# Split weights kept in DRAM for the second half, and every second sum of the second product on ScalarE in two convolution stages

## The chip, the core and the metric

The kernel runs on one core of one Trainium2 chip. The metric is the device time of that core in microseconds (us). Engines are called as in the profile: PE (TensorE), PEld (its weight loads), DVE (VectorE), ACT (ScalarE), POOL (GpSimd), SP (SyncE, which here only issues transfers).

## The reference

One sequence of S = 2048 rows of D = 576 channels. x is normalized by rows, and the output is x plus two branches of the normalized rows: a long convolution with gates (H3), and a two-layer network with ReLU whose hidden width is 4608.

```python
def A(q, k, v, shift_k, ssm_k, ssm_D):
    k_shift = sum of k shifted by 0..3 rows, each times a row of shift_k
    kv = k_shift * v
    y = irfft(rfft(pad(kv)) * rfft(pad(ssm_k)))[:S]     # along the rows, by channel
    return q * (y + kv * ssm_D)
def B(x, w1, w2):
    return relu(x @ w1) @ w2                            # 576 -> 4608 -> 576
xn = layernorm(A_q)
return A_q + A(xn, A_k, A_v, A_shift_k, A_ssm_k, A_ssm_D) + B(xn, B_w1, B_w2)
```

## The kernel before

**The network.** The rows are handled in two halves of 1024, each of two blocks of 512 (`HB` = 2) with four tiles of 128 rows (`BT` = 4). Each half runs over 18 chunks of 256 hidden columns (`NCHUNK`), so there are 36 chunks, `ci` 0 to 35, and chunk `ci` uses the same weights as chunk `ci + 18`. All products are of float32 numbers that are held as two parts, high and low (`hh` and `ll` for the hidden values); a product takes three matmuls: high x high, high x low, low x high.

The first product of a chunk is `quad` (chunks 0 and 18 take the plain form, `mm1`): it combines the four blocks of weights and x in the manner of Strassen and Winograd, in the banks `psk` (or `ka`), `pst` and `psa` of PSUM, and `relu` turns a finished bank into `hh` (on ACT) and `ll` (on DVE). The second product is `second`, run beside the next chunk's first product: for each of the two blocks one turn `mm2_rest` (4 matmuls of 512 columns, the last 64 output columns, transposed) and four turns `mm2` (6 matmuls each), ten turns a chunk. A turn takes one of the two banks of the pool `ps_o`, and DVE adds the finished bank to the sum held in SBUF (`accT` and `acc`). `DRAINS` says how many turns follow each step of `quad`.

**The weights of a chunk.** `prepare(ci)` runs one chunk ahead, in seven steps: DVE combines blocks of w1 (`combine_w`, four sums on the raw tile `r_`, lines 356 to 359); ACT rounds the main seven blocks to the high part and POOL subtracts for the low one (`split_main`, names `gah` and `gal`), then the same for two groups of the rest (`split_rest`, `gbh` and `gbl`) and two tiles of w2 (`split_w2`, `w_`). The raw loads of the next chunk stand after the fifth and the last step (`load_w1`, `load_w2`; one buffer each). All this is done in both halves.

**The convolution** is a generator, `conv`, of four stages: fk transforms the filter `ssm_k` (tile `kt`, loaded by 16 transfers), fx forms k, shift and v and transforms them (`tap`, `gate`, `split`), fm multiplies and transforms back along the other axis, from and to DRAM (`zk`, `zx`, `zy`), fo makes the last transform, the gate and the sum. Its matmuls have 288 columns and use the banks `psf`.

**Order.** PE's program sets the pace: after every third 512-column matmul `tick` advances a clock, and when the convolution's share is due it runs the stream on to its next `yield`. `yield -n` holds the stream back until n more matmul columns have been issued (16,000 columns, a `PAUSE`). `START` delays the stream's beginning, and `PAUSES` tells the rate how much holding back to reckon with. The program orders each engine's instructions by a model of their times, and places marked `issue_after` stay behind the named instruction: `here()` puts a convolution's step behind the last sum of the second product (`done["acc"]`) and the last activation (`done["act"]`).

**The start.** The four tiles of block 0 are loaded in two pairs; `first_xT` takes their statistics (BN_STATS, DVE), scales them (`normalized`) and transposes them on PE. `load_w1(0)` and `load_w2(0)` load chunk 0's weights; a part of them is held until the statistics of the first pair (`issue_after(seen.ins)`).

Of the kernel before, what the change touches and what calls it, by code (L numbers as in the profile page):

```python
# [10 lines left out]
F32 = mybir.dt.float32  # L11
# [6 lines left out]
P = 128  # L18
# [27 lines left out]
STEP = 3  # L46
DM = 512
DRAINS = (1, 1, 2, 1, 2, 2, 1)
SECOND = {(NCHUNK - 6, 0): 1, (NCHUNK - 4, 0): 0}
# [3 lines left out]
PAUSE = 16000  # L53
START = 24000
PAUSES = 24
SHARE = 0.985
# [61 lines left out]
def h3_ffn_kernel(ctx: ExitStack, tc, x, k, v, shift_k, ssm_k, ssm_D, w1, w2, fwd, inv, mid, out):  # L118
# [73 lines left out]
    def normalized(dst, src, t):  # L192
        nc.vector.tensor_scalar(dst, src, mv[:, t, 0:1], rstd[:, t:t + 1],
                                op0=OP.subtract, op1=OP.mult)

# [64 lines left out]
    def first_xT(srcs):  # L260

        plain_tiles(0)
        ps = []
        for c in range(5):
            ps.append(ps_o.tile([P, 512], F32, tag="o", name=f"psx{c}") if c >= 3 else fft_psum())
        xn = {}
        for t0 in range(0, BT, 2):
            pair = xp.tile([P, 2, D], F32, tag="xn", name=f"xn{t0}", bufs=BT // 2)
            for t in (t0, t0 + 1):
                seen = stats(t, srcs[t])  # L270
                xn[t] = pair[:, t % 2, :]
            if t0 == 0:
                with tc.issue_after(seen.ins):
                    load_w1(0, ((P, P),))
                    load_w2(0)
            inv_std(t0, 2)
            for t in (t0, t0 + 1):
                normalized(xn[t], srcs[t], t)
                for c in range(5):
                    w = min(P, D - c * P)  # L280
                    nc.tensor.transpose(ps[c][:w, t * P:(t + 1) * P], xn[t][:, c * P:c * P + w],
                                        ident)
                keep_warm(WARM_TILE[t])
        for c in range(5):
            split_x(0, c, ps[c])
# [59 lines left out]
    def load_w2(ci):  # L345
        f0 = (ci % NCHUNK) * FC
        r2 = wp.tile([P, FT, D], F32, tag="r2", name=f"r2_{ci}", bufs=1)
        nc.sync.dma_start(r2, w2[f0:f0 + FC, :].rearrange("(j p) d -> p j d", p=P))
        raw_w[2, ci] = r2
# [10 lines left out]

    def pair_of(tag, ci, n, bufs):
        return tuple(wp.tile([P, n, P], F32R, tag=f"{tag}{m}", name=f"{tag}{m}_{ci}", bufs=bufs)
                     for m in "hl")

    def split_main(ci):
        hi, lo = pair_of("ga", ci, 7, 2)
        src = raw_w[1, ci][:, :7, :]
        with at_turn(ci):
            nc.scalar.activation(hi, src, AF.Copy)  # L369
        split_lo(lo, src, hi)  # L370
        names = ("s1", "s2", "s3", "s4", "a12", "a22", "a11")
        weights[ci].update({n: (hi[:, k, :], lo[:, k, :]) for k, n in enumerate(names)})

    def split_plain(ci, j):
        if j == 0:
            weights[ci]["ga"] = pair_of("ga", ci, 7, 2)
        hi, lo = weights[ci]["ga"]
        src = raw_w[1, ci][:, 4 + j:8:2, :]
        to = slice(j, 4, 2)
        with at_turn(ci):  # L380
            nc.scalar.activation(hi[:, to, :], src, AF.Copy)
        split_lo(lo[:, to, :], src, hi[:, to, :])
        for k, n in ((j, "a12" if j == 0 else "a22"), (2 + j, "a11" if j == 0 else "a21")):
            weights[ci][n] = hi[:, k, :], lo[:, k, :]

    def split_rest(ci, j):
        hi, lo = pair_of("gb", f"{ci}_{j}", 3, 3)
        src = raw_w[1, ci][:, 8 + j::2, :]
        with at_turn(ci):
            nc.scalar.activation(hi, src, AF.Copy)  # L390
        split_lo(lo, src, hi)
        weights[ci]["r", j] = hi, lo

    def split_w2(ci, j):
        r2 = raw_w[2, ci]
        w = wp.tile([P, 2 * D], F32R, tag="w2", name=f"w2_{ci}_{j}", bufs=2 * FT)
        with at_turn(ci):
            nc.scalar.activation(w[:, :D], r2[:, j, :], AF.Copy)  # L398
# [3 lines left out]
        return last  # L402

    hid = {}
# [16 lines left out]
    def rest(ci, j, bi):  # L421
        hi, lo = weights[ci]["r", j]
# [58 lines left out]
    accT = {}  # L481

    def mm2_rest(ci, b):


        ps = ps_o.tile([P, 512], F32, tag="o", name=f"psr{ci}_{b}")
# [3 lines left out]
        if ci % NCHUNK == 0:  # L490
            accT[b] = xp.tile([P, 512], F32, tag="accT", name=f"accT{b}")
            done["acc"] = nc.vector.tensor_copy(accT[b], ps)
# [13 lines left out]
    def mm2(ci, b, i):  # L506
        t = b * BT + i
        cols = slice(i * P, (i + 1) * P)
        if ci == HALVES * NCHUNK - 1:
            while t not in added:  # L510
                next(stream)
        ps = ps_o.tile([P, 512], F32, tag="o", name=f"pso{ci}_{t}")
        seq = []
        for j in range(FT):
# [3 lines left out]
            seq += [(hh[:, cols], wh), (hh[:, cols], wl), (ll[:, cols], wh)]  # L518
        run_seq(ps, seq, True, True)
        last = ci == HALVES * NCHUNK - 1 and t == T - 1  # L520
        for d in range(2) if last else range(1):
            dc = slice(d * DM // 2, (d + 1) * DM // 2) if last else slice(0, DM)
# [34 lines left out]
    @contextmanager  # L557
    def here():


        with tc.issue_after(done["acc"].ins), tc.issue_after(done["act"].ins):
            yield

    def conv():

        with tc.tile_pool(name="fk", bufs=2) as fp:
            kt = fp.tile([P, NH, A2], F32, tag="kt", name="kt", bufs=1)  # L570
# [3 lines left out]
            for d in range(0, NH, KD):  # L574
                for h in range(2):
                    src = ssm_k[h * NH + d:h * NH + d + KD, :].rearrange("d (p t) -> p d t", t=A2)
                    nc.sync.dma_start(kt[halves(h)[0], d:d + KD, :], src)  # L577
                    yield -KT_GAP
# [33 lines left out]


        with tc.tile_pool(name="fx", bufs=2) as fp:
            sk = fp.tile([P, KS, D], F32, tag="sk", name="sk", bufs=1)
            for j in range(KS):
                nc.sync.dma_start(sk[:, j, :], shift_k[j:j + 1, :].to_broadcast([P, D]))
            win, gates, mats, sums, stks = {}, {}, {}, {}, {}
# [68 lines left out]


        with tc.tile_pool(name="fm", bufs=2) as fp:
            m_sb = fp.tile([P, 2, 2, P], F32R, tag="m", name="m_sb", bufs=1)  # L690
# [87 lines left out]


        with tc.tile_pool(name="fo", bufs=2) as fp:  # L780
            raw, parts, rest, ys = {}, {}, {}, {}
# [89 lines left out]


    stream = conv()
    clock = {"ffn": 0.0, "conv": 0.0, "until": START, "done": False}
# [50 lines left out]
    for j in range(FT):  # L925
        with tc.issue_after(done["act"].ins):
            done["pool"] = split_w2(0, j)
    load_w2(1)

    def prepare(ci):  # L930

        if ci >= HALVES * NCHUNK:
            while True:
                yield
        if ci % NCHUNK:
            combine_w(ci)
            yield
            split_main(ci)
        else:
            split_plain(ci, 0)  # L940
            yield
            split_plain(ci, 1)
        yield
        split_rest(ci, 0)
        yield
        split_rest(ci, 1)
        if ci + 1 < HALVES * NCHUNK:
            load_w1(ci + 1)
        yield
        split_w2(ci, 0)  # L950
        yield
        split_w2(ci, 1)
        if ci + 1 < HALVES * NCHUNK:
            load_w2(ci + 1)
        while True:
            yield

    def second(ci, half):
        for b in range(half * HB, (half + 1) * HB):
            mm2_rest(ci, b)  # L960
            yield
            for i in range(BT):
                mm2(ci, b, i)
                if i == 0 and ci % NCHUNK == NCHUNK - 1:
                    turn_back(b)
                yield

# [88 lines left out]
```

## Time and profile before

| | |
|---|---|
| median of 3 runs | 1173.7 us (1173.07 to 1176.47) |
| the profiled execution | 1176.29 us |
| its span, first to last instruction | 1174.5 us |
| mean granted clock of PE | 0.976 |
| busy: PE, DVE, ACT, POOL | 94%, 77%, 54%, 27% of the span |
| bytes by DMA | 151.81 MB |

A busy time is the time in which an engine has an instruction at work, and PE counts as busy also when its clock is throttled; "granted clock" is the share of full speed that it had. A line of waits reads: engine, tile and line of the instruction that waited, then what ended its wait, then total us, number, longest. In a line of single instructions the first column is the start in us, the second the duration, and what stands in brackets is the idle time before it and what ended it. A group of instructions reads: tile written and tiles read, shape out and in, count, then busy us and mean ns of one, then idle time before them and what ended most of it.

### The profile page before, as it was taken

To read this page: it belongs to the slowest core of one execution; us is meant where nothing else is said; L and a number is where in the kernel's file an instruction comes from. 1 tells how busy PE (TensorE), PEld (TensorE's weight loads), DVE (VectorE), ACT (ScalarE), POOL (GpSimd) and SP (SyncE) were. 2 spreads that over 40 slices of the span, in tenths; PEclk is the share of its full clock that TensorE was granted. 3 is DMA by queue.
4 is the path that set the end of the run, shared out by engine and by line. 5 is a ranking of instruction groups with operands and counts; after the bars stand their busy time and mean duration, and the time that the engine had idled before them with its cause. 6 is when DMAs were issued, how large, how long until landed. Compare 5 with 4: busy or idle time off the path is not lost.

```text
span 1174.5 us, 15018 instructions
## 1 busy us (share of the span) xinstructions
PE 1099.6 (94%) x5011; PEld 891.4 (76%) x5011; DVE 904.9 (77%) x1461; ACT 637.3 (54%) x1293; POOL 321.0 (27%) x328
## 2 busy tenths in 40 slices
PE   7799999998989999899999999999999998799997
PEld 5478888886767777678778888888788876578785
DVE  4844888768999989895777777777777765998985
ACT  2332677743434333324268887877788784544430
POOL 3233333322133333322132222221222221324520
PEclk8899999999899999999999999999999999899999
DMA  9941355464444445323464433434433424745723
GB/s 182 167 122 43 112 159 149 147 180 135 143 141 141 123 134 145 115 64 122 127 185 117 124 104 116 126 89 124 113 102 114 124 83 129 224 142 146 206 72 80
DMA packets 121016, 151.81 MB, mean 129 GB/s; under 512 B 46093, under 2 KB 71439, under 8 KB 120940
## 3 DMA queue, kind: packets, MB, share of 16 engines
q1 hardware_dynamic: 112652, 136.69, 42.3%
q0 software_dynamic: 7968, 13.44, 4.4%
q10 hardware_dynamic: 320, 0.74, 0.3%
q8 instruction: 39, 0.64, 0.2%
q14 instruction: 37, 0.30, 0.1%
HBM read 115.44 MB, written 35.39 MB: 128 GB/s over the span
## 4 chain that ended last, share of the span: by engine, by line
PE 58%; DVE 21%; ACT 7%; issue 5%; DMA 4%; SPq 3%; POOL 0%; DVEq 0%; ACTq 0%; POOLq 0%
PE pso L411 22%; PE psk L411 11%; PE psa L411 8%; PE pst L411 7%; PE psf L718 4%; PE psr L411 3%; DVE acc L523 3%; SPq L577 2%; DVE e L642 2%; DMA r<-in_w 2%; PE psf L554 2%; DVE ll L433 2%; DVE c L643 1%; DVE k L767 1%; ACT hh L432 1%
## 5 line engine op out<-in xcount | busy, mean ns | idle before, releaser
L411 PE MATMUL pso<-w,hh 128*128 128x512 f32 x1152 | 371.2, 402 | 38.0 <-DVE acc L523 28.4
L411 PEld LDWEIGHTS pso<-w,hh 128*128 128x128 f32 x1152 | 211.1, 191 | 91.3 <-DVE acc L523 38.4
L523 DVE TENSOR_TENSOR acc<-pso,acc 128x512 f32<-128x512 f32 x289 | 196.1, 681 | 51.8 <-PE pso L411 49.9
L411 PE MATMUL pso<-w,ll 128*128 128x512 f32 x576 | 229.3, 398 | 0.0
L324 POOL TENSOR_TENSOR gbl<-r,gbh 128x384 fp32r<-128x384 f32 x72 | 80.2, 1114 | 341.2 <-ACT gbh L390 332.9
L324 POOL TENSOR_TENSOR w<-r,w 128x512 fp32r<-128x512 f32 (+1 forms) x144 | 125.8, 904 | 162.6 <-ACT w L398 162.5
L411 PEld LDWEIGHTS pso<-w,ll 128*128 128x128 f32 x576 | 110.0, 191 | 23.8
L324 POOL TENSOR_TENSOR gal<-r,gah 128x896 fp32r<-128x896 f32 (+1 forms) x38 | 78.0, 2053 | 142.0 <-ACT gah L369 113.8
L548 DVE TENSOR_TENSOR ks<-kt,ks 64x288 fp32r<-64x288 f32 x64 | 49.2, 768 | 21.7 <-ACT ks L547 19.0
L369 ACT ACTIVATE gah<-r 128x896 fp32r<-128x896 f32 x34 | 32.4, 953 | 60.1 <-DVE r L359 59.9
L411 PE MATMUL psr<-hh,w 128*128 128x512 f32 x144 | 58.6, 407 | 5.7 <-DVE acc L523 4.8
L433 DVE SCALAR_TENSOR_TENSOR ll<-psk,hh 128x512 fp32r<-128x512 f32 x68 | 46.6, 685 | 21.3 <-ACT hh L432 21.0
L494 DVE TENSOR_TENSOR accT<-psr,accT 128x512 f32<-128x512 f32 x68 | 46.5, 684 | 19.4 <-PE psr L411 19.3
L411 PE MATMUL psr<-ll,w 128*128 128x512 f32 x144 | 58.4, 405 | 2.0 <-DVE ll L433 2.0
L432 ACT ACTIVATE hh<-psk 128x512 fp32r<-128x512 f32 x68 | 40.5, 595 | 30.8 <-PE psk L411 17.1
L709 DVE TENSOR_TENSOR lox<-ztx,hix 128x576 fp32r<-128x576 f32 x32 | 26.1, 817 | 39.4 <-ACT hix L708 39.4
L411 PE MATMUL psk<-xh,gbh 128*128 128x512 f32 x136 | 53.5, 393 | 0.0
L411 PE MATMUL psk<-xh,gbl 128*128 128x512 f32 x136 | 53.5, 393 | 0.0
L411 PE MATMUL psk<-xl,gbh 128*128 128x512 f32 x136 | 53.5, 393 | 0.0
L547 ACT ACTIVATE ks<-kt 64x288 fp32r<-64x288 f32 x64 | 47.3, 739 | 8.3 <-DVE kt L587 7.0
L398 ACT ACTIVATE w<-r 128x576 fp32r<-128x576 f32 x72 | 46.1, 676 | 6.3 <-DMA r<-in_w 4.0
L432 ACT ACTIVATE hh<-psa 128x512 fp32r<-128x512 f32 x35 | 20.8, 595 | 47.3 <-PE psa L411 47.0
(263 smaller groups left out, 2625.1 us busy)
## 6 DMA issues: line engine op xcount, KB each, us to landing
r<-in_w SPq DMA_DIRECT2D x36, 576.0 KB, 4.3
r<-in_w SPq DMA_DIRECT2D x35, 512.0 KB, 4.2
zk<-zk SPq DMA_DIRECT2D x32, 288.0 KB, 3.1
zx<-zx SPq DMA_DIRECT2D x32, 288.0 KB, 3.0
ztk<-zk SPq DMA_DIRECT2D x32, 288.0 KB, 2.8
ztx<-zx SPq DMA_DIRECT2D x32, 288.0 KB, 3.3
zy<-vo SPq DMA_DIRECT2D x32, 288.0 KB, 2.5
zo<-zy SPq DMA_DIRECT2D x32, 288.0 KB, 3.4
```

Of the source, the lines that this page charges most:

```text
L324: return nc.gpsimd.tensor_tensor(dst, src, hi, OP.subtract)
L369: nc.scalar.activation(hi, src, AF.Copy)
L398: nc.scalar.activation(w[:, :D], r2[:, j, :], AF.Copy)
L411: nc.tensor.matmul(ps, a, m, start=start and i == 0, stop=stop and i == len(seq) - 1, skip_group_check=not start)
L432: done["act"] = nc.scalar.activation(hh, ps, AF.Relu)
L433: lows.append(nc.vector.scalar_tensor_tensor(ll, ps, 0.0, hh, op0=OP.max, op1=OP.subtract))
L494: done["acc"] = nc.vector.tensor_tensor(accT[b], ps, accT[b], OP.add)
L523: done["acc"] = nc.vector.tensor_tensor(acc[t][:, dc], ps[:, dc], acc[t][:, dc], OP.add)
L547: nc.scalar.activation(dst[own], src[own], AF.Copy)
L548: nc.vector.tensor_tensor(dst[other], src[own], dst[own], OP.subtract)
L709: nc.vector.tensor_tensor(lo, raw[name, g], hi, OP.subtract)
L718: nc.tensor.matmul(ps[:, :NH], a, m[:, cols], start=n == 0, stop=n == 2)
```

## The change

Four things are changed.

1. **Kept weights.** In the first half each chunk's split weights are stored to DRAM (`kept_a`, `kept_b`, `kept_2`; five transfers a chunk on SP's queue, high and low part together, for which the tiles of the two parts become one tile). In the second half `prepare` loads them back (`fetch`), and `combine_w`, the splits and the raw loads fall away there.
2. **Seeds.** In the stages fx and fo (`SEEDED`), in all chunks but the first and last of a half, every second turn of the second product doesn't end in a sum by DVE: `prime` has ACT copy the sum from SBUF into the bank ahead of the matmuls, which add to it, and ACT copies the bank back. A turn's bank is taken one turn earlier.
3. **The filter's loads** are held back: each of the 16 has a memset of one column of its tile on DVE ahead of it, under `here()`. `START` falls from 24,000 to 8,000 columns and `PAUSES` rises from 24 to 25; the pause between fx's first loads and their use grows from 3 to 4 `PAUSE`, and these loads are put in another order (row of `sk`, then tile of k, by turns).
4. **The start.** The statistics of the second pair of tiles come after the scaling of the first (`issue_after(scaled.ins)`), and the held-back part of chunk 0's loads has three memsets of single columns ahead of it in place of `issue_after(seen.ins)`.

```diff
+SEEDED = ("fx", "fo")
-START = 24000
-PAUSES = 24
+START = 8000
+PAUSES = 25
...
+    kept_a = dram.tile([NCHUNK, P, 2, 7, P], F32, name="kept_a")
+    kept_b = dram.tile([NCHUNK, FT, P, 2, 3, P], F32, name="kept_b")
+    kept_2 = dram.tile([NCHUNK, FT, P, 2 * D], F32, name="kept_2")
...
-                seen = stats(t, srcs[t])
+                with tc.issue_after(scaled.ins) if t0 else nullcontext():
+                    stats(t, srcs[t])
...
-                with tc.issue_after(seen.ins):
-                    load_w1(0, ((P, P),))
-                    load_w2(0)
+                nc.vector.memset(raw_w[1, 0][:, 5, 0:1], 0.0)
+                nc.vector.memset(raw_w[1, 0][:, 13, 0:1], 0.0)
+                load_w1(0, ((P, P),))
+                load_w2(0)
...
+    def keep_main(ci):
+        n = 7 if ci else 4
+        nc.sync.dma_start(kept_a[ci, :, :, :n], f32(weights[ci]["ga"])[:, :, :n])
+    def keep_rest(ci):
+        for j in range(FT):
+            nc.sync.dma_start(kept_b[ci, j], f32(weights[ci]["r", j]))
+    def keep_w2(ci):
+        for j in range(FT):
+            nc.sync.dma_start(kept_2[ci, j], f32(weights[ci]["w2", j]))
+    def fetch(ci):
+        c0 = ci - NCHUNK
+        weights[ci] = {}
+        t = main_tile(ci)
+        n = 7 if c0 else 4
+        nc.sync.dma_start(f32(t)[:, :, :n], kept_a[c0, :, :, :n])
+        name_main(ci, t)
+        for j in range(FT):
+            yield
+            weights[ci]["r", j] = rest_tile(ci, j)
+            nc.sync.dma_start(f32(weights[ci]["r", j]), kept_b[c0, j])
+        for j in range(FT):
+            yield
+            weights[ci]["w2", j] = w2_tile(ci, j)
+            nc.sync.dma_start(f32(weights[ci]["w2", j]), kept_2[c0, j])
...
+    def seeded(ci):
+        return 0 < ci % NCHUNK < NCHUNK - 1 and stage[0] in SEEDED
+    def prime(ci, n):
+        b, i = ci // NCHUNK * HB + n // (BT + 1), n % (BT + 1)
+        ps = ps_o.tile([P, 512], F32, tag="o", name=f"pso{ci}_{b}_{i}")
+        seed = seeded(ci) and n % 2 == 1
+        if seed:
+            src = accT[b] if i == 0 else acc[b * BT + i - 1][:, :DM]
+            nc.scalar.activation(ps, src, AF.Copy)
+        turns[ci, n] = ps, seed
...
-        run_seq(ps, seq, True, True)
+        run_seq(ps, seq, not seed, True)
...
+        if seed:
+            done["act"] = nc.scalar.activation(acc[t][:, :DM], ps, AF.Copy)
+        for d in range(2) if last else range(0) if seed else range(1):
...
+                    with here():
+                        nc.vector.memset(kt[halves(h)[0], d:d + 1, 0:1], 0.0)
                     nc.sync.dma_start(kt[halves(h)[0], d:d + KD, :], src)
                     yield -KT_GAP
...
-            for t in range(1 - KS, 2):
-                load(t)
-            yield -3 * PAUSE
+            for j in range(KS):
+                nc.sync.dma_start(sk[:, j, :], shift_k[j:j + 1, :].to_broadcast([P, D]))
+                load(-j)
+            load(1)
+            yield -4 * PAUSE
...
     def prepare(ci):
-        if ci % NCHUNK:
+        if ci < NCHUNK:
             combine_w(ci)
+            keep_rest(ci - 1)
             yield
             split_main(ci)
             yield
             split_rest(ci, 0)
+            keep_w2(ci - 1)
             yield
             split_rest(ci, 1)
             if ci + 1 < NCHUNK:
                 load_w1(ci + 1)
             yield
             split_w2(ci, 0)
+            keep_main(ci)
             yield
             split_w2(ci, 1)
             if ci + 1 < NCHUNK:
                 load_w2(ci + 1)
+        elif ci < HALVES * NCHUNK:
+            ...
+            yield from fetch(ci)
```

How the instructions then stand is shown at three places. A row names line, operation, tile written and tiles read (the number behind a name tells one tile from the next), shape, and the count where rows of one kind follow each other.

First SP's queue of transfers at the start, behind chunk 0's weights. `acc` are rows of x, `kt` and `skip` the filter, `r_1` the raw weights of chunk 1. Before:

```order
L162 DMA acc_231<-in_x 64x1152 x2
L162 DMA acc_234<-in_x 64x1152 x2
L573 DMA skip<-in_ssm_D 1x288 x2
L577 DMA kt<-in_ssm_k 64x36x32 x11
L340 DMA r_1_237<-in_w 128x4x256
L342 DMA r_1_237<-in_w 64x256 x2
L577 DMA kt<-in_ssm_k 64x36x32 x2
L348 DMA r_1_249<-in_w 128x2x576
```

and now, with chunk 0's split weights (`ga_`, `gb_`, `w_0`) stored as well:

```order
L166 DMA acc_237<-in_x 64x1152 x2
L642 DMA skip<-in_ssm_D 1x288 x2
L429 DMA kept_b<-gb_0_136 128x768
L425 DMA kept_a<-ga_133 256x1x512
L346 DMA r_1_240<-in_w 128x4x256
L348 DMA r_1_240<-in_w 64x256 x2
L429 DMA kept_b<-gb_1_231 128x768
L433 DMA kept_94<-w_0_0_244 128x1152
L356 DMA r_1_253<-in_w 128x2x576
L433 DMA kept_94<-w_0_1_248 128x1152
L648 DMA kt<-in_ssm_k 64x36x32 x5
```

The raw weights of chunk 1 stood behind eleven of the filter's loads and now stand ahead of all of them, behind two stores.

Second ACT in stage fx, in chunk 10's first product. `hh` are the hidden values' high parts, `gbh`, `gah` and `w_10` (now `ga`, `gb`, `w_10`) the weights' splits, `zx` copies out of the convolution's banks. Before:

```order
L432 ACTIVATE hh_0_0_2925<-psk_2892 128x512
L390 ACTIVATE gbh_0_3011<-r_11_2799 128x384
L398 ACTIVATE w_10_0_2855<-r_10_2634 128x576
L398 ACTIVATE w_10_1_2886<-r_10_2634 128x576
L555 ACTIVATE zx_0_2834<-psf 128x288 x2
L555 ACTIVATE zx_1_2909<-psf 128x288 x2
L369 ACTIVATE gah_2977<-r_11_2799 128x896
L432 ACTIVATE hh_0_1_3033<-psa 128x512
```

and now:

```order
L480 ACTIVATE hh_0_0_2985<-psk_2952 128x512
L417 ACTIVATE w_10_0_2913<-r_10_2685 128x576
L588 ACTIVATE acc_237<-pso_1_4_2901 128x512
L417 ACTIVATE w_10_1_2946<-r_10_2685 128x576
L623 ACTIVATE zx_0_3048<-psf 128x288 x2
L543 ACTIVATE pso_0_1_2958<-acc_98 128x512
L623 ACTIVATE zx_1_3129<-psf 128x288 x2
L543 ACTIVATE pso_0_3_3020<-acc_101 128x512
L588 ACTIVATE acc_98<-pso_0_1_2958 128x512
L480 ACTIVATE hh_0_1_3097<-psa 128x512
L588 ACTIVATE acc_101<-pso_0_3_3020 128x512
L389 ACTIVATE ga_3055<-r_11_2856 128x896
```

Two copies into a bank of `pso` (L543) and three back (L588) came in between the hidden values' rows, and the main weight split (L389) moved behind the last of these.

Third DVE in stage fo, in chunk 31. `y` and `ll` belong to the convolution's last transform and to the hidden values, `r_32` is the raw tile that `combine_w` works on, `acc` the sum of the second product. Before:

```order
L859 TENSOR_TENSOR y_9230<-psf,low_1_9277 64x288
L433 SCALAR_TENSOR_TENSOR ll_0_0_9746<-psk_9705,hh_0_0_9745 128x512
L356 TENSOR_TENSOR r_32_9598<-r_32_9598 128x128
L357 TENSOR_TENSOR r_32_9598<-r_32_9598 128x128
L523 TENSOR_TENSOR acc_5253<-pso_15_9680,acc_5253 128x512
L469 TENSOR_TENSOR psk_9705<-psa,e_31_9778 128x512
L358 TENSOR_TENSOR r_32_9598<-r_32_9598 128x128
L859 TENSOR_TENSOR y_9230<-psf,low_1_9277 64x288
```

and now:

```order
L933 TENSOR_TENSOR y_9499<-psf,low_0_9500 64x288
L481 SCALAR_TENSOR_TENSOR ll_0_0_9591<-psk_9548,hh_0_0_9590 128x512
L514 TENSOR_TENSOR pst_9617<-psa,e_31_9621 128x512
L933 TENSOR_TENSOR y_9499<-psf,low_1_9552 64x288 x2
L559 TENSOR_TENSOR accT_5375<-pso_2_0_9565,accT_5375 128x512
L903 SCALAR_TENSOR_TENSOR acc_5332<-y_9400,rstd,acc_5332 128x576
L887 TENSOR_TENSOR olo_9609<-zo_9510,ohi_9608 128x576
L895 SCALAR_TENSOR_TENSOR y_9499<-xt_9329,mv,y_9499 128x576
L517 TENSOR_TENSOR psk_9548<-psa,e_31_9621 128x512
```

The rows of `r_32` are gone, and of the second product's sums only `accT` (L559) stands in this stretch; the convolution is a little further on.

More of the change, by code (lines that the diff above doesn't have):

```diff
@@ L421, in rest @@
     def rest(ci, j, bi):
-        hi, lo = weights[ci]["r", j]
+        hi, lo = (weights[ci]["r", j][:, m] for m in range(2))
         xh, xl, xr = plain[bi]
@@ L511, in mm2 @@
                 next(stream)
-        ps = ps_o.tile([P, 512], F32, tag="o", name=f"pso{ci}_{t}")
+        ps, seed = turns.pop((ci, b % HB * (BT + 1) + 1 + i))
         seq = []
@@ L558, in here @@
     def here():
-        with tc.issue_after(done["acc"].ins), tc.issue_after(done["act"].ins):
+        with tc.issue_after(done.get("acc", lows[-1]).ins), tc.issue_after(done["act"].ins):
             yield
     def conv():
+        stage[0] = "fk"
         with tc.tile_pool(name="fk", bufs=2) as fp:
```

118 lines of the change are left out of this document (67 added, 51 removed).

## The prediction, before the changed kernel was run

> **What bounds the kernel now.** I read the page first, then busy time by stretch, then PE's waits, then the timeline at the longest of them.
>
> ```profile
> span 1174.5 us, 15018 instructions
> PE 1099.6 (94%) x5011; PEld 891.4 (76%) x5011; DVE 904.9 (77%) x1461; ACT 637.3 (54%) x1293; POOL 321.0 (27%) x328
> ```
>
> PE is the busiest by far, so what counts is the time in which it isn't at full pace. The stretches (busy us of PE, PEld, DVE, ACT, POOL; then granted clock, DMA share, GB/s):
>
> ```profile
> 0.00:100.00 100.00, 85.06 (x336) 62.14 (x337) 54.94 (x119) 28.85 (x54) 29.89 (x36) 0.90 0.88 143
> 100.00:250.00 150.00, 148.54 (x693) 122.58 (x692) 112.07 (x168) 104.03 (x187) 47.14 (x52) 1.00 0.42 129
> 250.00:600.00 350.00, 318.79 (x1384) 254.87 (x1384) 297.84 (x461) 122.63 (x235) 97.72 (x96) 0.97 0.44 131
> 600.00:950.00 350.00, 345.25 (x1707) 291.67 (x1706) 262.62 (x423) 280.42 (x611) 84.73 (x75) 1.00 0.41 119
> 950.00:1150.00 200.00, 183.22 (x820) 146.28 (x819) 165.09 (x262) 101.36 (x208) 61.49 (x71) 0.97 0.50 141
> 1150.00:1174.50 24.50, 18.79 (x81) 13.81 (x79) 12.30 (x31) 0.00 (x0) 0.00 (x0) 0.99 0.36 96
> 300.00:350.00 50.00, 44.27 (x176) 34.75 (x177) 45.94 (x65) 18.41 (x35) 9.97 (x10) 0.90 0.49 151
> 350.00:400.00 50.00, 45.38 (x202) 36.15 (x201) 45.78 (x62) 18.21 (x36) 18.55 (x17) 1.00 0.39 121
> 1050.00:1100.00 50.00, 47.72 (x219) 38.93 (x220) 46.66 (x78) 24.45 (x48) 18.94 (x22) 1.00 0.64 175
> 1100.00:1150.00 50.00, 49.80 (x228) 40.71 (x227) 41.68 (x66) 17.88 (x36) 17.59 (x22) 1.00 0.33 99
> ```
>
> Lost PE time = idle + (1 - clock) x length: start 14.9 + 10 = 24.9; stage fk (100 to 250) 1.5; fx and the change of halves (250 to 600) 31.2 + 10.5 = 41.7; fm (600 to 950) 4.8; fo (950 to 1150) 16.8 + 6 = 22.8; tail 5.9. Together 101.6 us. The last three rows say where it comes from: with DVE at 45.8 or 46.7 of 50 us, PE idles 4.6 or 2.3; with DVE at 41.7 it idles 0.2; in fm, DVE at 37.5 of 50, it idles 0.7. The waits (total us, times, longest) name DVE too:
>
> ```profile
> PE pso L411 <- DVE acc L523: 28.4, 27, 2.5
> PE psr L411 <- DVE acc L523: 4.8, 1, 4.8
> ```
>
> The PE work itself, the same 3,955 matmuls of 512 columns (the code's counts, with the warming ones) and 960 of 288, doesn't change: starts stand 0.23 and 0.13 us apart at full pace, so about 3,955 x 0.233 + 960 x 0.133 + 6 for transposes = 1055 us.
>
> ```profile
> 985.79 0.29 PE L718 MATMUL psf<-yl,m_sb 128*128 128x288 f32 x1
> 985.92 0.30 PE L718 MATMUL psf<-yh,m_sb 128*128 128x288 f32 x1
> ...
> 986.32 0.39 PE L411 MATMUL psa<-t3h,gah 128*128 128x512 f32 x1
> 986.55 0.40 PE L411 MATMUL psa<-t3l,gah 128*128 128x512 f32 x1
> ```
>
> So each edit is worth what it takes out of the 101.6 us, at the stretch in which it acts, less what it adds.
>
> **The start.** Two things stand there.
>
> ```profile
> 1.09 0.06 DVE L907 MEMSET table<- 128x1 f32 x1
> 6.29 1.54 DVE L178 BATCH_NORM_STATS2 bn<-acc 128x6 f32<-128x288 f32 x4 [5.14 <-DMA acc<-in_x]
> ...
> 10.59 1.18 DVE L178 BATCH_NORM_STATS2 bn<-acc 128x6 f32<-128x288 f32 x3 [2.52 <-DMA acc<-in_x]
> 13.67 1.05 DVE L193 TENSOR_SCALAR xn<-acc,mv,rstd 128x576 f32<-128x576 f32 x2
> 14.38 0.87 PE L281 MATMUL psf<-ident,xn 128*128 128x128 f32 x3 [5.00 <-DVE xn L193]
> ...
> 18.24 0.63 PE L281 MATMUL psx<-ident,xn 128*128 128x128 f32 x2
> 20.46 19.43 SPq L577 DMA_DIRECT2D kt<-in_ssm_k  x8
> 40.08 1.98 SPq L340 DMA_DIRECT2D r<-in_w  x1
> 53.19 1.26 ACT L398 ACTIVATE w<-r 128x576 fp32r<-128x576 f32 x2 [4.00 <-DMA r<-in_w]
> 55.00 0.77 DVE L239 TENSOR_TENSOR t2l<-va,t2h 128x512 fp32r<-128x512 f32 x1 [2.74 <-ACT t2h L238]
> 56.75 1.22 PE L411 MATMUL pso<-w,hh 128*128 128x512 f32 x2 [4.01 <-DVE accT L492]
> ```
>
> (1) The first tiles are scaled only after the statistics of the late second pair (10.59). Now they are scaled before those, and PE transposes them early. The second pair's statistics take 1.5 from 10.59, and the small rows to its scaling 1.9 (from 11.77, the end of the statistics row, to 13.67 now); so its transposes start near 14.6 and, at about 1.1 us for each of two tiles, end near 16.8, not at 18.9: 2 us. The three memsets on the weights' tiles cost nothing: in the built order they stand ahead of everything that waits, so they hold no load back. (2) Eleven of the filter's loads stand on SP's queue ahead of chunk 1's weights, which were issued at 40.1; ACT waited for them until 53.2, DVE for ACT, PE for DVE. With each filter load behind a one-column memset on DVE (16 of 0.06 us, 1 us in all, spread over three chunks), chunk 1's weights are issued when their buffer is free, some 15 us earlier. That takes away DVE's 2.7 us and with it 3 of the 4.0; of the 10 us that the clock of 0.90 cost over this stretch I count 4 as given back. Start: 24.9 - 2 - 3 - 4 = 16. The filter loads now end nearer to their use (fk starts 16,000 columns, 7 us, earlier): 1 us more in fk, 2.5.
>
> **Kept weights.** First half: 5 stores a chunk, 2.9 MB, 51.5 MB in all; second half the same bytes back instead of 22.4 MB raw. 151.8 now + 103 - 22.4 = 232 MB, over 1131 us 205 GB/s. In fx that is 131 + 92 = 223 GB/s; at the 0.44 that 131 cost, 0.75 of the DMA engines. Nothing in the trace goes above 0.64 at 175 outside the start, so the landing time is bounded by 4.3 us (now) and 7.0 (the filter's, at the start's load); I take 5.
>
> ```profile
> DMA packets 121016, 151.81 MB, mean 129 GB/s; under 512 B 46093, under 2 KB 71439, under 8 KB 120940
> ...
> r<-in_w SPq DMA_DIRECT2D x36, 576.0 KB, 4.3
> kt<-in_ssm_k SPq DMA_DIRECT2D x16, 288.0 KB, 7.0
> ```
>
> Raw weights are issued about a chunk, some 30 us, ahead of their use (the code loads chunk n + 1 in chunk n - 1's last parts), so 1 to 3 us more there hide. Stores on SP wait for POOL's splits; behind them stand the next raw loads, which waited for the same splits before. Removed in the second half: ACT's and POOL's splits, and on DVE `combine_w` (L356 to L359), cheap alone (0.3 us), not beside POOL:
>
> ```profile
> 1000.24 3.40 DVE L357 TENSOR_TENSOR r<-r 128x128 f32<-128x128 f32 x1
> 1004.29 0.80 PE L411 MATMUL psr<-hh,w 128*128 128x512 f32 x1 [4.81 <-DVE acc L523]
> ```
>
> This one held the sum behind it, and PE 4.8 us. In fm nothing waits on DVE, so there it buys nothing: 4.8 becomes 5.
>
> **Every second sum by ScalarE.** 94 turns (57 while fx, 37 while fo, by the built order): off DVE 94 x 0.68 = 64 us, on ACT 94 x (one copy out + one copy in).
>
> ```profile
> L523 DVE TENSOR_TENSOR acc<-pso,acc 128x512 f32<-128x512 f32 x289 | 196.1, 681 | 51.8 <-PE pso L411 49.9
> L456 ACT ACTIVATE psa<-psk 128x512 f32<-128x512 f32 x34 | 19.8, 582 | 33.7 <-PE psk L411 33.6
> L708 ACT ACTIVATE hik<-ztk 128x576 fp32r<-128x576 f32 x32 | 21.9, 686 | 0.7
> ```
>
> No row writes PSUM from SBUF; 0.58 (PSUM to PSUM) to 0.69 (SBUF, 576 wide) bound it, I take 0.6. ACT gets 8 turns x 1.2 = 10 us in 50 and stands at 28 in fx; at 40 in fm it delayed PE by nothing that shows. On PE's path: a seeded turn needs copy out, copy in and two hand-overs, about 1.5 us, where a DVE turn needed about 1; one turn of PE between them is 6 x 0.233 = 1.4. In the built order about one seeded turn in ten stands that close: 0 (all hidden) to 94 x 0.3 = 28 us; I take 4 in fx and 2 in fo, near the lower end, since most have two turns or more between.
>
> fx: at its entry DVE waited for late loads, and PE for DVE:
>
> ```profile
> 267.37 0.76 DVE L642 TENSOR_TENSOR e<-k-1_2048,sk 128x576 f32<-128x576 f32 x1 [5.10 <-DMA k-1_2048<-in_k]
> 272.44 0.54 PE L411 MATMUL psk<-b11h,gah 128*128 128x512 f32 x1 [4.22 <-DVE ll L433]
> ```
>
> One PAUSE more between loads and use, 7 us, covers the 5.1: -4.2, and 1.4 of clock, in this stretch's own proportion (10.5 to 31.2). The other 36: DVE falls from 45.8 to 45.8 - 8 x 0.68 = 40.4 per 50, below the row that idles 0.2. Ends: 1 and 36; POOL's splits still stretch DVE's small ones here, and the change of halves is as it was, so 16. With the seeds 20 instead of 41.7.
> fo: 165 of DVE less 31 x 0.68 = 21 (the seeds that fall in this stretch) and about 10 of `combine_w` and its stretching leave 134 in 200, less than fm's share; fm's rate gives 3, the hand-over from fm 4, the seeds 2: 9 instead of 22.8.
>
> Sum: 16 + 2.5 + 20 + 5 + 9 + 5.9 = 58.4, 43 less. Span 1174.5 - 43 = 1131.5. The profiled execution took 1176.3, 2.6 over the median of the runs, 1173.7; from that median, **1131 us**.
>
> A rule to weigh: in the row of 300 to 350 the clock is 0.90, 5 us lost, although no wait in that row is longer than the 2.5 us that head the list; so I let the clock's loss fall only as the idle time falls. [...]
>
> **Rivals.** (a) ACT as a new link: ACT serves its queue in order, so a seed sits behind a copy that waits for PE or a load. For it: ACT already stands still for DVE, as in its weight splits:
>
> ```profile
> L369 ACT ACTIVATE gah<-r 128x896 fp32r<-128x896 f32 x34 | 32.4, 953 | 60.1 <-DVE r L359 59.9
> ```
>
> If each of 94 costs 0.3 us: 28 - 6 more, 1153. (b) fx's waits stay, because the order puts DVE's sums behind other long rows just as before: only start, entry and fo gain, 9 + 5.7 + 14 - 1 = 28: 1146. (c) Everything behind DVE goes (fx 6, fo 5): 1113. (d) Slower: SP issues in order, and a fetch of w2 must wait until the second product has let go of its buffer; the z rows of fm queue behind it. They are loaded two of fm's 32 groups (2 x 350 / 32 = 22 us) ahead and land in 3, so it bites only if a fetch holds the queue over 19 us; then PE waits each chunk. It decides from 43 / 11 = 4 us in each of fm's 11 chunks; at 6 the time is 1131 + 66 = 1197. Against it: the buffer has a whole chunk (350 / 11 = 32 us) to come free.
>
> **Numbers.** Forecast (1122 to 1140) 0.45; (a) 0.14; (b) 0.17; (c) 0.16; (d) 0.06; 0.02 for a gain and a loss that meet. Range 1108 to 1157, which holds (a) to (c) with their spread; out are (d) and half of the rest. Faster by over 0.3% (3.5 us, about what these runs can tell) 0.92, same 0.02, slower 0.06.
>
> **What would show it.** DVE near 40 in 50 us and PE idle under 2 in the middle of fx; `pso` waits on DVE under 15 us in all, with a new row of `pso` on ACT's copies under 10; first `psk` of chunk 1 near 54, not 59.5; no 3 us rows of r; fm's PE at 345 of 350. Wrong would be: ACT as releaser of pso with over 20 us, psf waiting for z's loads, or DVE still at 45 with PE waiting.

## The result, and the profile after

The changed kernel took 1158.7 us (median of 4 runs, 1156.7 to 1160.0) against 1173.4 before, a ratio of 0.987 (0.9845 to 0.9895): 14.6 us less, a third of the 43 that were forecast, and 1.7 us above the forecast range. The profiled execution took 1158.1 us.

The page's head, then busy time by the stretches of the prediction (columns as there):

```profile
span 1156.3 us, 15076 instructions
PE 1089.0 (94%) x5011; PEld 887.7 (77%) x5011; DVE 799.8 (69%) x1318; ACT 687.9 (59%) x1390; POOL 184.3 (16%) x201
```

```profile
0.00:100.00 100.00, 84.80 (x339) 62.13 (x340) 61.09 (x139) 29.47 (x55) 29.90 (x36) 0.91 0.91 218
100.00:250.00 150.00, 141.84 (x653) 116.63 (x652) 104.97 (x154) 105.66 (x191) 45.64 (x49) 0.99 0.72 235
250.00:600.00 350.00, 329.98 (x1468) 264.94 (x1467) 270.68 (x421) 177.38 (x337) 91.63 (x84) 0.99 0.71 227
600.00:950.00 350.00, 348.29 (x1738) 295.77 (x1737) 237.10 (x383) 272.96 (x604) 0.00 (x0) 1.00 0.52 170
950.00:1150.00 200.00, 182.96 (x817) 147.67 (x816) 124.74 (x221) 102.44 (x206) 17.11 (x32) 0.94 0.59 177
1150.00:1156.30 6.30, 1.08 (x5) 0.56 (x3) 1.19 (x3) 0.00 (x0) 0.00 (x0) 0.76 0.68 187
950.00:1000.00 50.00, 34.27 (x145) 27.25 (x144) 28.89 (x50) 30.57 (x65) 3.90 (x8) 0.76 0.72 208
```

Lost PE time, idle + (1 - clock) x length as in the prediction:

| | start | fk | fx | fm | fo | tail | sum |
|---|---|---|---|---|---|---|---|
| before | 24.9 | 1.5 | 41.7 | 4.8 | 22.8 | 5.9 | 101.6 |
| forecast | 16 | 2.5 | 20 | 5 | 9 | 5.9 | 58.4 |
| measured | 24.2 | 9.7 | 23.5 | 1.7 | 29.0 | 6.7 | 94.8 |

The span fell by 18.2, this sum by 6.8. The other 11 us lie in time that counts as busy: outside the sum stood 1174.5 - 101.6 = 1072.9 us, now 1061.5, against 1055 of pure work. A clock is shown to two digits, and 0.005 of 350 us is 1.7 us; reckoned over the whole span (clock 0.976, then 0.977) the sum falls by 9. So 9 to 11 of the 18 us are in no term of the forecast, and what they are is open. Without them the kernel would stand near 1168 to 1170 us; that the time comes as near to the range as it does is luck. DVE was relieved at least as far as forecast (270.7 in fx, 124.7 in fo). What PE now waits for:

```profile
PE psf L930 <- DMA xt<-in_x: 8.6, 1, 8.6
PE psa L459 <- DVE pst L514: 6.3, 3, 3.8
PE pso L459 <- DVE acc L591: 6.3, 12, 1.6
PE pso L459 <- ACT pso L543: 6.2, 8, 2.3
```

The sum on DVE (`pso` for `acc`), 28.4 before, is down to 6.3, and ACT's seeds hold PE for 6.2: rival (a) is small. The first two rows are new.

**The hand-over from fm to fo.** PE's timeline, then the transfers (SP's queue, one of POOL's) and the split of `zo`:

```profile
959.74 0.44 PE L791 MATMUL psf<-yh,m_sb 128*128 128x288 f32 x1
968.79 1.06 PE L930 MATMUL psf<-ohi,wi 128*128 128x288 f32 x3 [8.61 <-DMA xt<-in_x]
...
976.84 0.63 PE L459 MATMUL pso<-hh,w 128*128 128x512 f32 x1
```

```profile
956.32 4.65 SPq L850 DMA_DIRECT2D zy<-vo  x2
962.94 1.27 SPq L866 DMA_DIRECT2D zo<-zy  x3
963.64 1.59 POOL L872 DMA_DIRECT2D wi<-in_inv  x3 [430.77 <-DMA zy<-vo]
964.26 2.39 SPq L166 DMA_DIRECT2D xt<-in_x  x4
965.96 1.36 ACT L886 ACTIVATE ohi<-zo 128x576 fp32r<-128x576 f32 x2 [5.33 <-DMA zo<-zy]
```

fm's last matmul, the copy of its bank, the store of `zy`, fo's loads behind it and fo's first matmul are one chain, and PE had nothing else. The split was not the last link: its first high part was done at 966.6, 2.1 us before the matmul. The trace names the load of `xt`, which this matmul doesn't read; it reads `wi`, whose loads went out behind the same store at 963.6 and took 3.2 to 6.6 us to land (median 5.2). The network's next matmul comes at 976.84, after waiting for nothing: it stood behind fo's first ones. In PE's built order, the end of fm, fo's beginning and chunk 29's first turn:

```order
L791 MATMUL psf<-yh_8860,m_sb 128x288
L930 MATMUL psf<-ohi_9084,wi_8928 128x288 x2
...
L930 MATMUL psf<-ohi_9250,wi_9127 128x288
L459 MATMUL pso_2_0_9278<-hh_0_0_9044,w_29_0_8965 128x512
```

35 convolution matmuls stand in a row there; before the change 26 of the network's stood between the two stages. Of the 56 matmuls of chunk 29's second product, 50 stood ahead of fo's first matmul in the order before, and none does now. With the clock at 0.76 these 50 us lost 15.7 idle + 12 by the clock.

**fk.** Transfers on SP, DVE, and ACT around the wait of 3.8 us:

```profile
100.10 4.64 SPq L648 DMA_DIRECT2D kt<-in_ssm_k  x2
104.83 1.71 SPq L346 DMA_DIRECT2D r<-in_w  x1
```

```profile
111.11 0.29 DVE L364 TENSOR_TENSOR r<-r 128x128 f32<-128x128 f32 x1 [5.18 <-DMA kept_b<-gb]
...
111.72 0.69 DVE L514 TENSOR_TENSOR pst<-psa,e 128x512 f32<-128x512 f32 x1
```

```profile
111.46 0.52 ACT L409 ACTIVATE gb<-r 128x384 fp32r<-128x384 f32 x1 [5.09 <-DMA r<-in_w]
```

Raw weights of chunk 3 are issued at 104.8 and used by DVE's `combine_w` at 111.1 and ACT at 111.5; `pst`, which PE needs, stands behind `combine_w` on DVE.

**The start.** DVE, then ACT:

```profile
10.18 0.17 DVE L191 RECIPROCAL q<-q 128x2 f32<-128x2 f32 x1 [1.88 <-ACT q L190]
...
11.31 1.75 DVE L197 TENSOR_SCALAR xn<-acc,mv,rstd 128x576 f32<-128x576 f32 x2
12.98 1.52 DVE L182 BATCH_NORM_STATS2 bn<-acc 128x6 f32<-128x288 f32 x4
...
16.01 1.07 DVE L197 TENSOR_SCALAR xn<-acc,mv,rstd 128x576 f32<-128x576 f32 x2
```

```profile
9.64 0.42 ACT L401 ACTIVATE ga<-r 128x256 fp32r<-128x256 f32 x1 [6.15 <-DMA r<-in_w]
```

ACT's square root came 1.9 us late: it stood in ACT's queue behind this split of `ga`, which waited for raw weights until 9.6, and ran at 9.96. So the first pair was scaled at 11.3, and the second pair's statistics, there since 10.6, stood behind that. Its scaling is at 16.0, not earlier than before (15.2).

### The profile page after: what moved, and what is told of

Same layout as the page of the kernel before. It is cut to its first block, busy times and chain, and to the rows that moved or that the text cites. A ratio compares the mean times of both kernels' runs of the same rounds, so it can differ in the third digit from the quotient of the medians.

```text
span 1156.3 us, 15076 instructions
## 1 busy us (share of the span) xinstructions
PE 1089.0 (94%) x5011; PEld 887.7 (77%) x5011; DVE 799.8 (69%) x1318; ACT 687.9 (59%) x1390; POOL 184.3 (16%) x201
## 4 chain that ended last, share of the span: by engine, by line
PE 76%; DVE 10%; ACT 6%; DMA 6%; issue 2%; SPq 1%; DVEq 0%; ACTq 0%; POOL 0%; POOLq 0%
PE pso L459 33%; PE psk L459 12%; PE psa L459 11%; PE pst L459 9%; PE psf L791 6%; PE psf L622 2%; DMA zk<-zk 2%; PE psh L459 1%; DVE e L712 1%; DVE acc L591 1%; DVE c L713 1%; DVE ll L481 1%; ACT ks L615 1%; DMA r<-in_w 1%; DMA v<-in_v 1%
## 5 line engine op out<-in xcount | busy, mean ns | idle before, releaser
L459 PEld LDWEIGHTS pso<-w,hh 128*128 128x128 f32 x1152 | 210.0, 189 | 66.9 <-DVE acc L591 10.7
L591 DVE TENSOR_TENSOR acc<-pso,acc 128x512 f32<-128x512 f32 (+1 forms) x214 | 146.2, 683 | 69.0 <-PE pso L459 67.5
L459 PE MATMUL psk<-xh,gb 128*128 128x512 f32 x272 | 97.2, 393 | 0.0
L588 ACT ACTIVATE acc<-pso 128x512 f32<-128x512 f32 x75 | 44.9, 598 | 72.6 <-PE pso L459 71.9
L330 POOL TENSOR_TENSOR w<-r,w 128x512 fp32r<-128x512 f32 x72 | 66.6, 955 | 84.8 <-ACT w L417 73.2
L616 DVE TENSOR_TENSOR ks<-kt,ks 64x288 fp32r<-64x288 f32 x64 | 48.4, 756 | 29.2 <-ACT ks L615 27.7
L459 PE MATMUL pso<-ll,w 128*128 128x512 f32 x144 | 57.3, 398 | 3.3 <-DVE ll L481 3.3
L459 PE MATMUL pso<-hh,w 128*128 128x512 f32 x144 | 57.7, 401 | 2.0 <-ACT pso L543 1.5
L480 ACT ACTIVATE hh<-psk 128x512 fp32r<-128x512 f32 x68 | 40.5, 596 | 31.1 <-PE psk L459 23.8
L459 PEld LDWEIGHTS psk<-xh,gb 128*128 128x128 f32 x272 | 50.9, 188 | 10.6
L481 DVE SCALAR_TENSOR_TENSOR ll<-psk,hh 128x512 fp32r<-128x512 f32 x68 | 46.5, 684 | 15.7 <-ACT hh L480 15.5
L543 ACT ACTIVATE pso<-acc 128x512 f32<-128x512 f32 x75 | 44.8, 597 | 16.5 <-DVE acc L591 11.7
L459 PE MATMUL psk<-xl,gb 128*128 128x512 f32 x136 | 53.4, 393 | 0.0
L459 PE MATMUL psa<-xh,gb 128*128 128x512 f32 x140 | 50.1, 394 | 0.0
L459 PE MATMUL pst<-xh,gb 128*128 128x512 f32 x136 | 49.4, 402 | 0.0
```

What stands on the lines that cost most here:

```text
L330: return nc.gpsimd.tensor_tensor(dst, src, hi, OP.subtract)
L459: nc.tensor.matmul(ps, a, m, start=start and i == 0, stop=stop and i == len(seq) - 1, skip_group_check=not start)
L480: done["act"] = nc.scalar.activation(hh, ps, AF.Relu)
L481: lows.append(nc.vector.scalar_tensor_tensor(ll, ps, 0.0, hh, op0=OP.max, op1=OP.subtract))
L543: nc.scalar.activation(ps, src, AF.Copy)
L588: done["act"] = nc.scalar.activation(acc[t][:, :DM], ps, AF.Copy)
```

## The experiments

All were timed in 3 rounds beside the kernel before (1172.7). S is the changed kernel with seeds in fx alone. The changed kernel and runs 1, 3 and 9 have the same code up to fo's first seed at 890 us, and run 2 has it up to fx's first at 208. In these profiles the start lost 24.1 to 26.0, fk 8.2 to 12.7, and fx, where its code is the same, 20.4 to 23.5, so differences inside that are not read.

**1. Seeds in fx alone (S).**

```diff
-SEEDED = ("fx", "fo")
+SEEDED = ("fx",)
```

> Seeds in stage fx alone (SEEDED holds fx only). Theory A (the built order at the hand-over from fm to fo): with seeds in fo the network's ten turns of chunk 29 stand on PE behind the first 16 matmuls of fo, so PE stands still for fo's first loads and then runs at half clock, some 20 us in all; without them the order has the turns between, and the time falls from 1158.7 to about 1143 (1139 to 1148), although DVE then makes all sums in fo. Theory B (the kept weights' transfers delay fo's loads of zo and xt, whatever the order): the wait of 8.6 us stays and the time is 1156 to 1161. Theory C (seeds in fo are worth what the prediction said, some 14 us, and the hand-over is something apart): 1165 or more.

Measured 1147.0 us (1144.0 to 1149.2), 11.7 less. fk, the whole behind 950 us, and the hand-over:

```profile
100.00:250.00 150.00, 141.85 (x641) 116.39 (x639) 104.76 (x153) 104.35 (x190) 45.20 (x49) 0.97 0.71 231
...
950.00:1143.10 193.10, 178.82 (x821) 144.33 (x819) 143.55 (x252) 71.69 (x147) 17.07 (x32) 1.00 0.65 193
950.00:1000.00 50.00, 43.79 (x205) 34.83 (x203) 33.17 (x57) 25.61 (x54) 3.71 (x7) 1.00 0.78 232
```

6.2 lost in the 50 us of the hand-over instead of 27.7, with more traffic (232 GB/s against 208): theory A, not B. In PE's built order 27 of the network's matmuls stand between the two stages again.

**2. No seeds.** `SEEDED = ()`.

> No seeds at all, everything else as changed. Theory A: fo gains as in the run with seeds in fx alone, and what seeds bring in fx (of the 19 us that stretch 250 to 600 lost less) is lost again: 1152 to 1163. If the seeds bring nothing in fx, and the gain there is from the later use of its first loads and the filter's, it equals the run with seeds in fx alone, about 1143. Theory C: above 1170.

1153.9 (1150.1 to 1155.2). Against S, seeds in fx bring 6.9 us. fx without and with them:

```profile
250.00:600.00 350.00, 326.13 (x1441) 260.70 (x1440) 299.59 (x465) 121.85 (x231) 87.46 (x84) 0.99 0.69 224
```

```profile
250.00:600.00 350.00, 332.72 (x1484) 267.21 (x1483) 268.96 (x422) 178.40 (x340) 92.36 (x85) 0.99 0.71 229
```

30.6 us less of DVE are worth 6.6 of PE by these two rows, 4 to 7 by the scatter of fx among the kernels above. Of the 41.7 that fx lost before the change, 14.3 are gone without any seed.

**3. A longer pause at fo's entry, seeds in fx and fo.** In it one tile's addition by fo falls between a seed and its copy back and is lost; the work is the same.

```diff
-            yield -3 * PAUSE
+            yield -5 * PAUSE
```

> Seeds in fx and fo as changed, but fo's first loads stand 5 pauses ahead of their use, not 3. In the built order the network's matmuls then stand between fm's last and fo's first matmul again. Theory A: the wait of 8.6 us and most of the half clock go, and DVE keeps its relief in fo: 1137 to 1146, unless fo, which starts later, holds up the last chunk. Theory B: the loads are late because of the traffic, a longer pause hides it as well, but the wait of loads by themselves (issue to landing) stays at 6 us or more, and the time is 1140 to 1158.

1146.0 (1145.7 to 1146.2). The order at the hand-over is mended by another means (26 of the network's matmuls stand between the stages), and the same time comes back. This time lies in the ranges of both theories. Theory B's sign, a landing of 6 us or more, is there too (6.2 us median for fo's `xt` between 930 and 1010 us), but it was 7.2 in the kernel before, which had no such wait; so it does not speak for B, and runs 1 and 4 decide.

```profile
950.00:1000.00 50.00, 45.01 (x203) 37.35 (x202) 29.76 (x50) 29.88 (x64) 3.71 (x7) 0.91 0.82 245
```

**4. No kept weights, seeds in fx and fo.** `prepare` as before the change in both halves, no stores, no `fetch`.

> No kept weights: both halves load raw weights, combine and split them as before; nothing is stored or fetched; the other parts as changed. The built order has the same hand-over as the changed kernel (53 convolution matmuls in a row). Theory A: the wait at the hand-over stays, and DVE's and POOL's work in the second half comes back, which fm hides and fo partly: 1160 to 1170. Theory B: without the 103 MB more of traffic the hand-over's wait is gone: 1138 to 1150.

1171.5 (1169.4 to 1174.5); 1.5 above theory A's bound. The wait of 8.6 us stands there too (8.7), at 158 GB/s in place of 208, and the order is worse: 53 convolution matmuls stand in a row.

```profile
PE psf L930 <- DMA xt<-in_x: 8.7, 1, 8.7
```

```profile
950.00:1000.00 50.00, 32.37 (x119) 25.09 (x120) 29.90 (x48) 32.05 (x68) 8.39 (x10) 0.69 0.57 158
```

**5. S without kept weights.** The edits of 1 and 4.

> Seeds in fx alone, as in the run at 1147.0, and no kept weights. With that run it gives the worth of the kept weights where the hand-over to fo is in order. Theory D (the stores and the filter's loads together fill the DMA engines up to 110 us, so raw weights of chunk 3 land late and fk loses 7 to 9; later DVE's and POOL's relief brings 12 in fo and 5 in fm): the loss between 100 and 250 us falls from 13 to 4, those behind 600 us grow by 12 to 17, and the time is 1150 to 1157. Rival (the 12.8 us that keeping was worth beside the bad hand-over came from that alone): 1138 to 1144.

1158.2 (1157.2 to 1160.9), 1.2 above theory D's range; the rival's (1138 to 1144) is far off. With the hand-over in order, keeping is worth 11.2 us. By stretch, the run without:

```profile
100.00:250.00 150.00, 147.22 (x684) 120.78 (x682) 106.18 (x160) 109.92 (x200) 45.02 (x50) 1.00 0.45 135
250.00:600.00 350.00, 327.73 (x1454) 263.18 (x1454) 278.27 (x429) 186.14 (x360) 109.04 (x99) 0.98 0.48 138
```

fk loses 2.8 (the runs that store 8.2 to 12.7), so storing costs 5 to 10 there; fx loses 29.3 (S: 20.8), and what lies behind 950 us 29.9 (S: 14.3). The theory had the loss behind 950, not the 8.5 in fx, of which 5.5 fall in its first 50 us.

**6. S, chunks 0 to 3 not kept** (loaded and split again in the second half).

> Seeds in fx alone; chunks 0 to 3 aren't stored, and the second half loads, combines and splits these four again, the other 14 are kept. Theory D: without stores in the first 130 us the raw weights of chunk 3 come in time, the wait of 3.8 us near 112 and its half clock go, and the loss between 100 and 250 us falls from 13 to 4 or 5; the four chunks cost 1 or 2 behind 600 us: 1138 to 1141. Rival (chunk 3's raw weights stand on SP behind the filter's loads, which wait for their memsets under here(), with or without stores): no change, 1145 to 1149.

1142.4 (1141.1 to 1144.6), 4.7 less than S and 1.4 above theory D's range. fk loses 5.4 (S: 12.7), and from 100 to 120 us DMA is at 0.33 where it was at 0.98 in the changed kernel, and PE doesn't idle. Behind 950 us it loses 21.2 where S lost 14.3; 1 to 2 were expected there, and why it is more is open. This run, then the changed kernel:

```profile
100.00:250.00 150.00, 144.61 (x672) 119.02 (x671) 108.77 (x159) 109.82 (x200) 45.60 (x49) 1.00 0.64 219
100.00:120.00 20.00, 20.00 (x91) 16.47 (x90) 15.42 (x22) 10.99 (x19) 6.73 (x7) 1.00 0.33 121
```

```profile
100.00:120.00 20.00, 16.16 (x65) 12.84 (x64) 11.21 (x17) 6.55 (x10) 6.22 (x6) 0.91 0.98 289
```

The raw weights of chunk 3 in this run:

```profile
97.29 0.37 SPq L346 DMA_DIRECT2D r<-in_w  x1
```

They go out as soon as POOL has let go of their buffer, 7.5 us earlier than in the changed kernel (104.83), where the buffer was free at 96.5. There, stores of chunk 2's weights (from 90.65 on) and two filter loads (from 100.10 on) stand ahead of them on SP's queue. So most of their lateness is their place in that queue.

**7. S, the filter's loads not held back.** `START` 24,000, `PAUSES` 24, no memsets on `kt`.

> Seeds in fx alone, kept weights; the filter's loads as before the change: not held back, START 24,000 and PAUSES 24. The prediction's step (holding them back gives 7 us at the start, as chunk 1's weights come 15 us earlier): about 1154, 7 lost in the first 100 us. Theory D: with the filter's loads done by 60 us the stores have the DMA engines to themselves later, so fk's loss falls from 13 to 4 or 5 and the start loses 1 to 7 more: 1139 to 1146.

1151.2 (1150.7 to 1151.9), above theory D's range. The start loses 31.1 (S: 24.6), fk 3.1, but fx 35.4: PE waits 7.2 us at fx's entry for a `ll` behind late loads. Holding back is worth 5 to 7 at the start, costs 5 to 10 in fk, and shifts where fx's entry falls.

**8. S, the start as before.** Statistics and chunk 0's loads in the old order.

> Seeds in fx alone; the order of the first statistics and scalings as before the change (no issue_after(scaled), no three memsets, chunk 0's loads behind issue_after(seen)). The prediction's step: 2 us lost at the start, 1149. Reading of the changed kernel's trace (ACT's square root comes 1.9 us late, so the first pair is scaled at 11.3, the second pair's statistics stand behind that, and the last transpose ends no earlier): first 512-column matmul at 19.2 to 19.4 as in both kernels, 1146 to 1148.

1144.2 (1143.3 to 1144.2), if anything faster than S, and below both forecasts. The step is worth nothing.

**9. Seeds in the second half from chunk 30 on.** `... and not 18 < ci < 30` in `seeded`.

> The changed kernel, but in the second half only chunks 30 and later have seeds: chunks 28 and 29, whose turns stand at the hand-over from fm to fo, have none, the other seeds in fo (about 27) stay. The built order then has the network's matmuls between fm's last and fo's first. Theory A (all that the seeds of fo cost lies at the hand-over): the stretch 950 to 1000 us loses 8 to 10 and not 23, and the time is 1143 to 1149. If the remaining seeds also bring what the prediction gave them (DVE is the bound in fo): below 1140. If seeds in fo cost by themselves (ACT's copies late): 1152 or more.

1151.8 (1150.5 to 1153.0): between theory A and the cost by themselves. Most of the hand-over's loss is gone (27.7 to 10.7); then PE's wait for the seeds:

```profile
950.00:1000.00 50.00, 42.29 (x188) 34.03 (x187) 31.62 (x54) 25.75 (x54) 3.71 (x7) 0.94 0.77 233
```

```profile
PE pso L459 <- ACT pso L543: 9.3, 8, 2.2
```

In S, with fx's seeds alone, this wait was 4.8. The seeds that are left bring nothing, and cost some 5 against S; why here and not in run 3 is open.

**10. Run 6 with the stores' traffic but not their waits.**

> As the run that keeps chunks 4 to 17 (1142.4), with seeds in fx alone; in place of the stores of chunks 0 to 3 stand transfers of the same bytes from DRAM (rows of w1) to the same places in DRAM, at the same points of SP's queue, which wait for no split. Nothing reads them. Theory D (the bytes fill the DMA engines, so chunk 3's raw weights land late): the loss between 100 and 250 us is 10 to 13 as with the stores, and the time 1146 to 1150. Rival (SP's queue stands behind stores that wait for POOL's splits): that loss stays at 5 to 7 and the time at 1141 to 1144.

1148.6 (1145.9 to 1150.9): theory D's time. The place is another: the transfers go out earlier, and the loss is in the first 100 us (32.3, run 6: 25.1), where ACT stands 13.5 us for chunk 2's weights and PE then 6.1 for ACT, not in fk (4.4). So the stores' waits for the splits are not needed for a loss. That the bytes alone cost it is not shown: these transfers stand on SP's queue too, and chunk 2's raw weights go out 9 us later than in run 6 (63.98).

```profile
72.94 0.54 SPq L346 DMA_DIRECT2D r<-in_w  x1
```

```profile
78.95 0.52 ACT L409 ACTIVATE gb<-r 128x384 fp32r<-128x384 f32 x1 [13.51 <-DMA r<-in_w]
```

**11. Seeds in fx, chunks 3 to 17 kept, filter held back, the old start.**

> The parts that paid, together: seeds in fx alone, chunks 3 to 17 kept, the filter's loads held back, the start as before the change. By the stretches of the runs so far: fk 6 to 7 as with chunks 4 to 17 kept, fo 19 as with seeds in fx alone (the order at the hand-over is the one of that run), start 26 to 28: 1137 to 1142.

1139.8 (1135.3 to 1141.6), ratio 0.971 (0.969 to 0.973): the fastest. The time is as expected, the parts are not: the start loses 21.2, fk 5.1, fx 28.4 (S: 20.8) and what lies behind 950 us 15.3.

## Why the prediction was wrong

- **fo (9 forecast, 29.0).** The step that failed most is "the hand-over from fm 4, the seeds 2". I took the hand-over's cost from before and priced the seeds by durations; what they did was to move ten turns, nine of which had stood ahead, behind fo's first matmuls in PE's built order. Runs 1, 3 and 9 show it: three ways to restore the order turn the 27.7 of these 50 us into 6.2, 9.5 and 10.7. The order was there to be read before any run. DVE's relief in fo was at least what was said (124.7 busy, 134 forecast), but with `combine_w` gone DVE is no limit there (143.6 in S, and less lost). What in the builder's model makes it put the turns last is open.
- **fk (2.5 forecast, 9.7).** The step that failed is "behind them stand the next raw loads, which waited for the same splits before", which put the delay on SP's queue at nothing; "1 us more in fk" was all that was left. The raw weights of chunk 3 went out at 104.8 and not at 97.3 (run 6). That they take "5" to land was about right: w1's raw loads took 5.1 us (median of the run) and 6.2 up to 120 us, where it was 7.3 before the change. Run 5 takes all stores out, run 6 those of chunks 0 to 3, and run 7 the filter's loads (they are done earlier): fk loses 2.8, 5.4 and 3.1. Whether the bytes cost something beside the place in the queue is not shown. There are 27.5 MB up to 120 us, where 15.1 stood before. Transfers of the changed kernel up to 120 us:

```profile
DMA packets 46613, 27.53 MB, mean 229 GB/s; under 512 B 38063, under 2 KB 41265, under 8 KB 46606
```

- **Start (16 forecast, 24.2).** Step (1) failed because I let the first pair's scaling follow its statistics without ACT's square root (run 8: nothing lost without it). Step (2), 7 forecast: beside the stores, holding back the filter gives 5 to 7 (run 7), but against the kernel before it gave next to none. The stores aren't the reason: without them the start lost 24.2 and 21.6 (runs 4 and 5). The wait for loads did go (ACT had chunk 1's w2 at 48.1, not 53.2), but then DVE was busy without a break from 38 to 57, with rows stretched beside POOL's splits (47.4 to 53.5), as this one, which took 0.28 before. So `accT`, which PE waited for, was copied at 54.8 (56.0 before), chunk 1's first `psk` came at 58.2 (59.5 before, 54 forecast), and the clock gave back 1 of the 4 (0.91). In run 4 these two came at 54.6 and 58.0.

```profile
52.29 1.04 DVE L366 TENSOR_TENSOR r<-r 128x128 f32<-128x128 f32 x1
```

- **fx (20 forecast, 23.5).** About right in size, wrong in parts: seeds gave 4 to 7 (run 2), keeping 3.0 (run 4 against the changed kernel) to 8.5 (run 5 against S). "One PAUSE more covers the 5.1" failed: DVE still waited 5.4 us for its first load, which went out only at 255.7, behind fk's last store on SP's queue (252.7), and PE then waited 2.0. The sign for the middle of fx came true from 350 to 400 us (DVE 40.3, PE idle 0), not from 300 to 350 (42.6 and 5.7). DVE at fx's entry:

```profile
263.52 0.76 DVE L709 TENSOR_TENSOR c<-k,sk 128x576 f32<-128x576 f32 x1 [5.37 <-DMA k<-in_k]
```

- **fm (5 forecast, 1.7), copies and rival (d).** Nothing waits for z behind the fetches; SP waited up to 10.7 us for w2's buffer, inside the 19 us of slack. ACT's copies took 0.60 each way, as assumed. The wait on SP, then the copies:

```profile
SPq L450 <- PE pso L459: 51.2, 23, 10.7
```

```profile
L543 ACT ACTIVATE pso<-acc 128x512 f32<-128x512 f32 x75 | 44.8, 597 | 16.5 <-DVE acc L591 11.7 <-DVE accT L559 4.2
```

- **The clock.** From 300 to 350 us the clock is 0.97, 1.5 us lost, and the longest wait in that row is 2.4 us (`psk` for DVE's `ll`, until 315.3); from 317.0 to 320.4 us the clock is 0.50. At the hand-over it is 0.53 from 955 to 960, before the wait of 8.6, with no wait longer than 2.2 us up to 958.1. So the clock falls to half beside waits of 2.4 and 2.2 us, and in the trace of before, from 300 to 350 us, it was 0.90 beside waits of 2.5 at most; what brings it down is open. That its loss falls only as the idle time falls was an estimate, and fo does not bear it out: the idle time from 950 to 1150 us stayed (16.8, then 17.0), and the clock's loss rose from 6 to 12.

```profile
300.00:350.00 50.00, 44.30 (x193) 35.21 (x192) 42.58 (x59) 28.07 (x54) 15.30 (x14) 0.97 0.73 243
```

```profile
PE psk L459 <- DVE ll L481: 2.4, 1, 2.4
```

## What to carry to other kernels

Where a program's order is made by a builder's model, read the built order at every hand-over between stages before pricing anything: an edit made of copies of 0.6 us cost 12 us by moving other work behind a wait. Work that is taken off an engine need not pay where that engine isn't the limit, and two edits that relieve the same engine (here the seeds and the kept weights in fo) need not add up: with both and the order mended (run 3), DVE was busy for 126.7 us behind 950 us and PE lost 18.4; without the seeds in fo (S) it was 143.6 and 14.3. Before adding transfers, look at the stretch in which loads are already waited for, and leave that stretch out (chunks 0 to 2 in run 11). A transfer that is added to a queue can delay the loads that stand behind it: the raw weights of chunk 3 went out at 104.8 us and not at 97.3 (run 6); the stores landed in 4.8 to 5.6 us (medians).

## What was not expected of the hardware

The weights' landing times rose little with the traffic: 576 KB of raw w2 landed in 4.3 us at 129 GB/s over the span, and 576 KB of kept w2 in 5.1 at 201. Smaller loads rose more: `xt` from 3.0 to 3.9 us and k from 2.9 to 4.1 (144 KB each). In the first 100 us the engines' share was 0.91 at 218 GB/s, and 0.88 at 143 before the change, so a share near 0.9 did not mean there that no more bytes would pass. From 100 to 250 us 235 GB/s took 0.72. In the first 120 us 38,063 of 46,613 packets are under 512 B; that these make the difference is not shown.

```profile
w<-kept SPq DMA_DIRECT2D x36, 576.0 KB, 5.1
```
